# First attention in a fixed order, with row sums from a ones column, and chunks of three tiles, two of them from two batches

## The chip, the cores and the metric

One NeuronCore of one Trainium2 chip. The metric is device time in microseconds (us) of one execution, as the median over runs. TensorE is called PE, VectorE DVE, ScalarE ACT, GpSimd POOL and SyncE, whose queue issues most transfers, SP.

## The reference, cut to what matters

Attention over 4 batches, 8 heads, 768 positions and 64 columns a head, with a window of 128 positions and the first 4 positions as sinks; then a gated MLP without a nonlinearity on the 3072 resulting rows.

```python
scores = scale * np.matmul(q, k.transpose(0, 1, 3, 2))
keep = is_sink | in_window                    # in_window: 0 <= row - col < window
scores = np.where(keep, scores, -1000000000.0)
a = np.exp(scores - np.max(scores, axis=-1, keepdims=True))
a = a / (np.sum(a, axis=-1, keepdims=True) + 1e-09)
attn_out = np.matmul(a, v)                    # (4, 8, 768, 64)
x = attn_out.transpose(0, 2, 1, 3).reshape(B * S, H * D)          # (3072, 512)
return (x @ w_a) * (x @ w_b) @ w_out          # w_a, w_b: (512, 1536), w_out: (1536, 512)
```

The three weights arrive as 64-bit floats.

## The kernel before

The 3072 rows are 24 tiles of 128, six to a batch. The first tile of each batch (t = 0) sees only itself; a later one sees its own block, the block before it and the sinks. The work goes in passes. Ahead of all, `first_tiles` (L405) does the attention of the four first tiles. Then each pass of `moe` (L722) runs the MLP for the rows whose attention is finished, while the attention of the next chunk is fed in between its products, one step of a generator at a time (`between`, L818). `CHUNKS` (L216) lists those chunks as (batch, first tile, tiles); there are eight of 2 or 3 tiles, all of one batch, so there are nine passes: one on the four first tiles and eight on 2 or 3 tiles.

A pass goes over 12 values of j, 128 of the 1536 hidden columns each. For each j, `half` (L730) makes the a and b products, 12 each with as many moving columns as the pass has rows; ACT copies a out of its bank (L755), DVE multiplies it by b (L761), the product is split into a high and a low part (L764, L766), and one j later `project` (L740) adds it to the output banks with three products of 512 columns for each tile (L745). Everything is done in pairs of rounded high and low parts, three products for one, except the attention of the first tiles and of chunk 0 (`parts_exact`, L576), which takes full 32-bit products.

Weights are loaded in the first pass as raw 64-bit words and pass three steps: `weight_bits` (L296: DVE L301 and L303, ACT L302, POOL L305), `weight_high` (ACT L312) and `weight_low` (DVE L317). `weights_to` (L787) calls them one weight behind the other, the second step D1 = 3 weights behind the first and the third D2 = 4 behind it. It is called in `first_tiles` from its seventh `yield` on (nine calls) and three times for each j of the first pass, where at third s it brings the third step to at least s + 3 and goes one weight on at every call.

In `first_tiles`, for each batch: scores of eight heads by products on 64 rows (L417) and a mask product onto each of two banks (L420); the maximum by DVE (L429), the exponentials on ACT with an accumulated row sum (L432), the reciprocal and the scaling of the 512 columns of each half (L438 to L440), transposes (L445) and copies (L446), products with V (L453), and the split into xh and xl (L456, L457). The program's scheduler puts these into an order; instructions under `pin` (`keep_in_program_order`) keep theirs. Eight products on a zero tile (`warm`, L271) stand at the very start.

For a split chunk, `prep_kq` (L351) and `prep_v` (L370) load K, Q and V of a head (K and V for two heads at once) into a ring of six transfer buffers (`io`, L279, NIO = 6), and POOL rounds and subtracts (L343, L346). The weight checks (`check_weight`, L319) load through the same ring, two tiles for each j in which they run, from the third pass on. A buffer is given out again only when its last reader is done, and SP issues in order.

## Time and profile before

| what | us |
|---|---|
| median of 3 runs (823.36 to 824.60) | 824.04 |
| the profiled execution | 823.73 |
| its span, first to last instruction | 821.9 |
| first product of the first MoE pass | 47.87 |
| cut behind the first pass (first split of the next rows, L718) | 174.5 |

The profile of one execution shows each instruction with start and duration. The stages in the rows below are cut at the first MoE product and then at each `split_x` (L718), which starts when the attention of a chunk is finished; the last two projections of a pass still run behind its cut. A matmul's record includes its way through the array, so the records of neighbours overlap; the pace at which they follow each other stands in the chain of waits, which counts every product up to the next one's end.

### The profile page before, as it was taken

The numbers are of one execution on the slowest core, as the hardware profiler recorded it, in microseconds if no ns is written. First come the engines' busy times: TensorE is split into PE (matmuls) and PEld (weight loads), VectorE is DVE, ScalarE is ACT, GpSimd is POOL, SyncE is SP. The second block draws the span as 40 slices with busy tenths as digits, with TensorE's granted clock in tenths as the row PEclk, the third lists the DMA queues.
The fourth block names the chain that finished last, engine by engine and source line by source line (L and its number), as shares of the span: only waits on it lengthen the run. The fifth ranks groups of instructions, "written<-read, shape, count | busy, mean of one in ns | idle before, by whom it ended". The sixth has DMA issues, their size and how long they took to land.

```text
span 821.9 us, 14178 instructions
## 1 busy us (share of the span) xinstructions
PE 789.3 (96%) x4751; PEld 705.0 (86%) x4751; DVE 429.9 (52%) x1365; ACT 476.9 (58%) x1413; POOL 374.8 (46%) x499
## 2 busy tenths in 40 slices
PE   7688999999999999999999999999999999999997
PEld 4466777789889999999999888999998889999996
DVE  4799777426654565335534675355356643442211
ACT  3565666338865777457636886576368755652311
POOL 1244434707762665247363664473646725630110
PEclk7679999999999999999999999999999999999999
DMA  9907510322121332223331443133314211000100
GB/s 337 381 20 280 199 32 4 94 74 66 54 82 39 101 100 91 82 65 116 110 113 52 123 145 96 66 114 115 106 57 137 78 37 54 23 1 1 39 2 29
DMA packets 45662, 76.34 MB, mean 93 GB/s; under 512 B 4688, under 2 KB 25488, under 8 KB 45584
## 3 DMA queue, kind: packets, MB, share of 16 engines
q1 hardware_dynamic: 42384, 69.62, 26.5%
q10 hardware_dynamic: 3168, 5.77, 1.9%
q8 instruction: 38, 0.62, 0.3%
q14 instruction: 40, 0.33, 0.1%
q0 software_dynamic: 32, 0.00, 0.0%
HBM read 69.08 MB, written 6.29 MB: 92 GB/s over the span
## 4 chain that ended last, share of the span: by engine, by line
PE 72%; DVE 11%; ACT 9%; POOL 3%; issue 2%; DMA 2%; SPq 0%; ACTq 0%; POOLq 0%; DVEq 0%
PE b L736 20%; PE o L745 20%; PE a L736 19%; PE t L530 3%; PE s L501 3%; ACT p L508 2%; PE av L545 2%; ACT p L512 2%; DVE pt L534 1%; ACT pt L533 1%; ACT xf L550 1%; DVE xf L551 1%; PE s L417 1%; POOL ks L346 1%; DVE g L761 1%
## 5 line engine op out<-in xcount | busy, mean ns | idle before, releaser
L745 PE MATMUL o<-w_o,gh 128*128 128x512 f32 x576 | 188.2, 407 | 0.0
L736 PE MATMUL b<-xh,w_b 128*128 128x256 f32 (+1 forms) x768 | 186.5, 313 | 0.0
L736 PE MATMUL a<-xh,w_a 128*128 128x256 f32 (+1 forms) x768 | 184.9, 311 | 0.0
L766 POOL TENSOR_TENSOR gl<-g,gh 128x256 fp32r<-128x256 f32 (+1 forms) x80 | 70.2, 878 | 192.6 <-ACT gh L764 188.1
L761 DVE TENSOR_TENSOR g<-b,g 128x256 f32<-128x256 f32 (+2 forms) x108 | 55.4, 513 | 163.0 <-PE b L736 155.4
L736 PEld LDWEIGHTS a<-xh,w_a 128*128 128x128 f32 x768 | 132.3, 188 | 2.3
L736 PEld LDWEIGHTS b<-xh,w_b 128*128 128x128 f32 x768 | 132.3, 188 | 0.0
L736 PE MATMUL b<-xl,w_b 128*128 128x256 f32 (+1 forms) x384 | 118.6, 309 | 0.0
L736 PE MATMUL a<-xl,w_a 128*128 128x256 f32 (+1 forms) x384 | 118.4, 308 | 0.0
L745 PEld LDWEIGHTS o<-w_o,gh 128*128 128x128 f32 x576 | 102.0, 190 | 18.4 <-ACT gh L764 1.1
L745 PE MATMUL o<-w_o,gl 128*128 128x512 f32 x288 | 114.8, 399 | 0.0
L755 ACT COPY g<-a 128x256 f32<-128x256 f32 (+2 forms) x108 | 47.3, 438 | 105.0 <-PE a L736 89.4
L764 ACT CAST gh<-g 128x256 fp32r<-128x256 f32 (+2 forms) x108 | 51.7, 479 | 76.3 <-DVE g L761 74.7
L512 ACT ACTIVATE p<-p,st 128x264 f32<-128x264 f32 x144 | 74.4, 517 | 27.6 <-DVE st L511 27.5
L506 DVE CUSTOM_DVE_ANT_0 p<-s,mg 128x264 f32<-128x264 f32 x120 | 51.3, 427 | 54.0 <-PE s L501 53.4
L534 DVE TENSOR_TENSOR pt<-t,pt 128x256 fp32r<-128x256 f32 x144 | 60.8, 422 | 30.8 <-ACT pt L533 28.8
L508 ACT ACTIVATE p<-p,st 128x264 f32<-128x264 f32 x144 | 74.4, 517 | 3.8 <-DVE st L506 3.6
L736 PEld LDWEIGHTS a<-xl,w_a 128*128 128x128 f32 x384 | 72.3, 188 | 2.2
L736 PEld LDWEIGHTS b<-xl,w_b 128*128 128x128 f32 x384 | 72.3, 188 | 0.0
L346 POOL TENSOR_TENSOR ks<-kr,ks 64x536 fp32r<-64x536 f32 (+1 forms) x56 | 68.0, 1215 | 4.5
L745 PEld LDWEIGHTS o<-w_o,gl 128*128 128x128 f32 x288 | 54.5, 189 | 13.3
L533 ACT CAST pt<-t 128x256 fp32r<-128x256 f32 x144 | 53.4, 371 | 21.3 <-PE t L530 17.1
(153 smaller groups left out, 1424.3 us busy)
## 6 DMA issues: line engine op xcount, KB each, us to landing
raw_a<-in_wa_dram SPq DMA_DIRECT2D x12, 512.0 KB, 7.7
raw_b<-in_wb_dram SPq DMA_DIRECT2D x12, 512.0 KB, 7.8
raw_o<-in_wo_dram SPq DMA_DIRECT2D x12, 512.0 KB, 7.1
qr<-in_qT_dram SPq DMA_DIRECT2D x32, 192.0 KB, 2.8
chk_a<-in_wa_dram SPq DMA_DIRECT2D x24, 256.0 KB, 2.7
chk_b<-in_wb_dram SPq DMA_DIRECT2D x24, 256.0 KB, 2.6
chk_o<-in_wo_dram SPq DMA_DIRECT2D x24, 256.0 KB, 3.0
out_dram<-os ACTq DMA_DIRECT2D x22, 256.0 KB, 2.2
```

Source lines behind the costliest of these rows:

```text
L346: self.nc.gpsimd.tensor_tensor(o, i, high.bitcast(F32), op=ALU.subtract)
L506: nc.vector.tensor_tensor_reduce(out=p[:, :w], in0=ps[:, :w], in1=m, scale=-0.125, scalar=BIG, op0=ALU.add, op1=ALU.min, accum_out=st[:, 0:1])
L508: nc.scalar.activation(p[:, :w], p[:, :w], AF.Exp, bias=st[:, 0:1], scale=-1.0, accum_out=st[:, 1:2])
L512: nc.scalar.mul(p[:, :w], p[:, :w], st[:, 3:4])
L533: nc.scalar.copy(hs, tp[:, :n, :])
L534: nc.vector.tensor_tensor(ls, tp[:, :n, :], hs.bitcast(F32), op=ALU.subtract)
L736: nc.tensor.matmul(ps[:, :n], lhsT=w[:, ksl], rhs=x[:, kk, :n], start=kk == 0 and i == 0, stop=kk == NK - 1 and i == 2)
L745: nc.tensor.matmul(outs[i], lhsT=g[:, sl], rhs=w, start=j == 0 and k == 0, stop=j == NJ - 1 and k == 2)
L755: nc.scalar.copy(g[:, :n], pa[:, :n])
L761: nc.vector.tensor_tensor(g[:, :n], pb[:, :n], g[:, :n], op=ALU.mult)
L764: nc.scalar.copy(gh[:, :n], g[:, :n])
L766: e.tensor_tensor(gl[:, :n], g[:, :n], gh[:, :n].bitcast(F32), op=ALU.subtract)
```

## The change

The attention of the first tiles, `first_tiles`, is written out as one list of calls, and every instruction in it keeps that order. The row sums are no longer accumulated beside the exponentials: V gets two more columns (DA = 66) set to ones, the product is turned (the probabilities are loaded, V moves), its column 64 is the row sum, and the scaling is done on the 64 columns of the result, which then is transposed (`turn`). Twelve products on the zero tile are added (`busy`): two behind the first scores, two ahead of each of two turns, six at the end. K and Q of the next batch are loaded ahead of V of the one before; the ones are set by POOL behind V's transfer. The weights' steps get bounds of their own: in `first_tiles` three first steps, two second and two third; in the passes at third s the first step up to s + 7, the second up to s + 4, at most two at a call, the third up to s + 3. Chunks 1 to 6 have three tiles; the last two take two tiles of one batch and one of another, with K and V in pieces, one sink product for each piece, and eight products of V a head (`PAIR` and `LONE`) where a chunk of one batch has seven (`ROW`). The sink values are loaded at heads 3 and 7 instead of 0 and 4. Small tables share buffers with weights that come late.

The diff, cut to its core:

```diff
-MB = 4
-MK = MB * KB - NS
+MB = 5
+MK = MB * KB - 2 * NS
-CHUNKS = ((0, 1, 2), (0, 3, 3), (1, 1, 3), (1, 4, 2), (2, 1, 3), (2, 4, 2), (3, 1, 3), (3, 4, 2))
+SLOTS = ((0, 4, "BA"), (1, 2, "AB"), (3, 5, "AB"))
+ROW = ((0, 0, 2, 0), (1, 2, 2, 1), (2, 5, 0, 2), (-1, 4, 1, 0))
+PAIR = ((0, 0, 2, 0), (1, 2, 1, 1), (-1, 4, 1, 0))
+LONE = ((0, 5, 0, 2), (-1, 3, 0, 2))
+CHUNKS = (((0, 1, 2),), ((0, 3, 3),), ((1, 1, 3),), ((2, 1, 3),), ((3, 1, 3),),
+          ((1, 4, 2), (2, 4, 1)), ((3, 4, 2), (2, 5, 1)))
+DA = D + 2
...
+    def prep_kq(self, places, h, tag):
+        if h % 2 == 0:
+            self.kr = []
+            for b, t0, n, s0, nb, kw, *_ in places:
+                kr = self.io([P, 4 * KB - NS], F32, f"kr{tag}_{h}_{b}")
+                self.nc.sync.dma_start(kr[:, :kw], self.kT[b, h // 2, :, s0 * KB:s0 * KB + kw])
+                self.kr.append(kr)
...
+        for b in range(B + 1):
...
+            if b:
+                nc.sync.dma_start(self.vs0[b - 1], self.v0[b - 1])
+                nc.gpsimd.memset(self.vs0[b - 1][:, :, D:], 1.0)
...
+        def busy(bank, n):
+            for _ in range(n):
+                pin(T.matmul(bank, lhsT=self.z[:, :P], rhs=self.z[:, :bank.free_size()], start=True, stop=True,
+                             skip_group_check=True))
...
+        def exps(b, e):
             for pr in range(NP):
-                A.activation(p[:, pr, :], s[:, pr, :], AF.Exp, bias=st[:, 1, pr:pr + 1], scale=0.125,
-                             accum_out=st[:, 2, pr:pr + 1])
+                pin(A.activation(ps[b][:, e, pr, :], banks[b][e][:, pr, :], AF.Exp,
+                                 bias=sts[b][:, 1, e, pr:pr + 1], scale=0.125))
...
         def av(b):
+            avs[b] = [tile(("av", "o2")[e], [P, NP, DA], f"av0_{b}_{e}") for e in range(2)]
+            for e in range(2):
+                for pr in range(NP):
+                    pin(T.matmul(avs[b][e][:, pr, :], lhsT=pts[b][:, e, pr, :], rhs=self.vs0[b][:, 2 * pr + e, :],
+                                 start=True, stop=True))
+
+        def scale(b):
+            st = sts[b]
+            for e in range(2):
+                pin(V.tensor_scalar(st[:, 2, e], avs[b][e][:, :, D], 1e-9, None, op0=ALU.add))
+            pin(V.reciprocal(st[:, 3], st[:, 2]))
+            for e in range(2):
+                pin(V.tensor_tensor(xs[b][:, :, e, :], avs[b][e][:, :, :D],
+                                    st[:, 3, e].unsqueeze(2).to_broadcast([P, NP, D]), op=ALU.mult))
+
+        def turn(b, n):
+            xts[b] = tile(("t", "s", "o0", "s")[b], [P, NP, P], f"xt0_{b}")
+            busy(xts[b].rearrange("p a b -> p (a b)"), n)
             for pr in range(NP):
+                pin(T.transpose(xts[b][:, pr, :], xs[b][:, pr].rearrange("p a b -> p (a b)"), self.ident))
...
+        scores(0)
+        busy(tile("t", [P, DM], "busy0"), 2)
+        mask(0)
+        top(0, 0)
+        top(0, 1)
+        scores(1)
+        mask(1)
+        exps(0, 0)
...
+        av(3)
+        scale(3)
+        turn(2, 2)
+        split(2)
+        between(2)
+        turn(3, 2)
+        busy(tile("t", [P, DM], "busy1"), 6)
+        split(3)
+        between(3)
...
+        def beside(k):
+            if k == 0:
+                weights(load=3, bits=1)
+            elif k == 1:
+                weights(load=9, bits=2, high=1)
+                next(gen)
+            elif k == 2:
+                weights(load=9, bits=2, high=2, low=1)
+            elif k == 3:
+                weights(load=9, bits=3, high=2, low=2)
...
             def ahead(s):
                 j = s // 3
-                weights_to(max(s + AHEAD, done[0] + 1 - D2), LOADS)
+                weights(load=s + LOADS + AHEAD, bits=min(s + AHEAD + D2, done["bits"] + 2),
+                        high=min(s + AHEAD + 1, done["high"] + 2), low=s + AHEAD)
```

## Rows read from the trace of the kernel before

**Rows 1.** The page: busy time, share of the span and instructions of each engine (part 1), and the clock that PE was granted in 40 equal slices, in tenths (part 2).

```profile
PE 789.3 (96%) x4751; PEld 705.0 (86%) x4751; DVE 429.9 (52%) x1365; ACT 476.9 (58%) x1413; POOL 374.8 (46%) x499
...
PEclk7679999999999999999999999999999999999999
```

**Rows 2.** The chain of waits, pieces in order of time: start in us, length in us, engine, tile, line and count. The first is of the pass on four tiles, the next two of a pass on three, the last two of the pass on two.

```profile
101.02 2.79 PE o L745 x12
...
340.27 2.08 PE a L736 x12
...
344.44 4.19 PE o L745 x18
...
765.59 1.41 PE a L736 x12
...
779.79 1.40 PE o L745 x6
```

**Rows 3.** Busy time of each engine in each stage, in us, with the count of instructions, the granted clock, the busy share of the transfer engines and GB/s. The first is the first attention, the next two the first MoE pass; 174.5 and 597.5 start passes on two tiles beside attention of three, 251.1 one on three beside three.

```profile
0.00:47.87 47.87, 33.34 (x176) 22.92 (x176) 30.65 (x76) 24.76 (x88) 10.54 (x17) 0.69 0.83 311
47.87:80.00 32.13, 29.30 (x113) 22.37 (x113) 31.14 (x53) 17.64 (x37) 15.54 (x13) 0.87 0.45 160
80.00:174.50 94.50, 93.25 (x438) 72.69 (x437) 60.58 (x135) 52.55 (x117) 39.65 (x40) 1.00 0.27 86
174.50:251.10 76.60, 74.40 (x535) 68.62 (x534) 43.25 (x160) 52.82 (x164) 46.24 (x62) 1.00 0.22 68
251.10:344.50 93.40, 93.17 (x551) 87.16 (x551) 49.13 (x176) 60.71 (x187) 47.16 (x62) 1.00 0.29 89
...
597.50:673.80 76.30, 73.48 (x528) 67.14 (x527) 44.19 (x177) 53.51 (x171) 44.52 (x62) 1.00 0.27 82
```

**Rows 4.** The timeline, instructions in order of time: start in us, length in us, engine, line, operation, result and sources, shape and count, and in brackets the idle time before it and what ended it.

```profile
4.81 1.20 PE L417 MATMUL s<-kq 64*128 64x128 f32 x16
...
5.99 0.35 DVE L265 SCALAR_TENSOR_TENSOR m<-col,nw_val,mg 128x128 bf16<-128x128 f32 x1
...
6.97 0.23 DVE L269 TENSOR_SCALAR mg<-rel,nw_val 128x8 f32<-128x8 f32 x1
...
10.46 1.65 PE L420 MATMUL s<-m,identb 128*128 128x512 bf16 x4
...
23.98 1.97 PE L453 MATMUL av<-pt,v 128*64 128x128 f32 x14
...
25.88 1.97 PE L445 MATMUL t<-ident,p 128*128 128x128 f32 x8
...
30.01 1.09 PE L453 MATMUL av<-pt,v 128*64 128x128 f32 x14
...
41.07 1.29 POOL L305 TENSOR_TENSOR wf_b<-wf_b,raw_b 128x512 int32<-128x512 int32 x1 [3.58 <-ACT raw_b L302]
...
44.72 0.69 DVE L303 SCALAR_TENSOR_TENSOR wf_o<-raw_o,wf_o 128x512 int32<-128x512 int32 x1
...
48.56 0.42 DVE L301 TENSOR_SCALAR wf_b<-raw_b 128x512 int32<-128x512 int32 x1
...
50.94 1.52 POOL L305 TENSOR_TENSOR wf_b<-wf_b,raw_b 128x512 int32<-128x512 int32 x1 [0.78 <-ACT w_a L312]
...
51.24 1.52 DVE L301 TENSOR_SCALAR wf_o<-raw_o 128x512 int32<-128x512 int32 x1
...
816.02 0.39 PE L745 MATMUL o<-w_o,gl 128*128 128x512 f32 x1
```

**Rows 5.** Groups of instructions by line and shape, here POOL's subtraction of K for a chunk of three tiles and one of two: count, busy us, mean ns of one, idle us before them.

```profile
L346 POOL TENSOR_TENSOR ks<-kr,ks 64x536 fp32r<-64x536 f32 x32 | 42.9, 1342 | 2.6
...
L346 POOL TENSOR_TENSOR ks<-kr,ks 64x400 fp32r<-64x400 f32 x24 | 25.1, 1046 | 1.9
```

**Rows 6.** The chain of waits at the start.

```profile
2.23 6.17 DMA kq<-in_kq_dram
...
8.45 2.08 PE s L417 x16
...
11.11 1.29 DVE st L429 x2
...
12.57 1.29 ACT p L432 x7
```

**Rows 7.** Groups by line and shape in the first attention, 0 to 47.87 us: count, busy us, mean ns of one, idle us before them.

```profile
L432 ACT ACTIVATION_READ_ACCUMULATOR p<-s,st 128x1 f32 x32 | 7.3, 227 | 0.0
...
L440 DVE TENSOR_TENSOR p<-p,st 128x512 f32<-128x512 f32 x8 | 6.4, 799 | 0.1
...
L429 DVE TENSOR_REDUCE st<-s 128x4 f32<-128x512 f32 x8 | 5.4, 686 | 5.3 <-PE s L420 5.3
...
L438 DVE TENSOR_SCALAR st<-st 128x4 f32<-128x4 f32 x8 | 1.2, 159 | 2.7 <-ACT p L432 2.7
```

**Rows 8.** Busy time of each engine in stretches of 4 us, with the granted clock (1.00 is 2.4 GHz, 0.50 is 1.2).

```profile
16.00:20.00 4.00, 4.00 (x16) 2.68 (x15) 3.09 (x10) 2.62 (x16) 0.00 (x0) 0.50 1.03 410
...
24.00:28.00 4.00, 4.00 (x24) 3.34 (x24) 2.44 (x6) 2.17 (x10) 0.00 (x0) 0.50 1.02 408
```

**Rows 9.** What SP's queue waited for in the pass from 251.1 to 344.5 us (us in total, times, longest), and then the transfers by line: KB each and median us from issue to landing.

```profile
SPq L333 <- POOL ql L346: 34.5, 6, 18.4
...
kr<-in_kT_dram SPq DMA_DIRECT2D x16, 268.0 KB, 2.7
```

More of the change, by code (lines that the diff above doesn't have):

```diff
@@ L33 @@
 NIO = 6
-STEP0 = 7
 AHEAD, LOADS = 3, 9
-D1, D2 = 3, 4
+D2 = 4
 WARM = 8
@@ L392, in first_inputs @@
[L392 to L394 removed]
+        self.kqs = [self.wp.tile([P, NP, 2, P], F32, tag=HOMES[b], name=f"kq{b}") for b in range(B)]
+        self.vs0 = [self.wp.tile([P, H, DA], F32, tag=HOMES[B + b], name=f"v0_{b}") for b in range(B)]
+        for b in range(B + 1):
             if b == 0:
@@ L459, in first_tiles @@
[L459 to L475 removed]
+            pin(A.copy(xh[:, :, cols], xts[b]))
@@ new lines, in split @@
+            pin(V.tensor_tensor(xl[:, :, cols], xts[b], xh[:, :, cols].bitcast(F32), op=ALU.subtract))
+        scores(0)
[6 more added lines that the diff above has]
+        exps(0, 0)
+        top(1, 0)
+        exps(0, 1)
+        transposes(0, 0)
+        top(1, 1)
+        exps(1, 0)
+        transposes(0, 1)
+        exps(1, 1)
+        scores(2)
+        mask(2)
+        top(2, 0)
+        top(2, 1)
@@ new lines, in first_tiles @@
+        av(0)
+        scale(0)
+        transposes(1, 0)
+        exps(2, 0)
+        between(0)
+        transposes(1, 1)
+        scores(3)
+        mask(3)
+        exps(2, 1)
+        top(3, 0)
+        top(3, 1)
+        turn(0, 0)
+        split(0)
+        av(1)
+        exps(3, 0)
+        scale(1)
+        transposes(2, 0)
+        transposes(2, 1)
+        exps(3, 1)
+        av(2)
+        turn(1, 0)
+        between(1)
+        scale(2)
+        transposes(3, 0)
+        transposes(3, 1)
@@ new lines, in first_tiles, with attention @@
+        split(1)
+        av(3)
[7 more added lines that the diff above has]
+        between(3)
+    def attention(self, segs, xf, exact=False):
+        tiles = [t0 + i for _, t0, n in segs for i in range(n)]
+        nt = len(tiles)
+        late = [i for i, t in enumerate(tiles) if t >= 2]
+        parts = self.parts_exact(*segs[0], xf) if exact else self.parts_split(segs, tiles, late, xf)
@@ L840, in run @@
                     pass
-                rows = [nb * S + (nt0 + i) * P for i in range(nnt)]
-                xs = self.split_x(nxf, nnt, f"{rows[0]}")
+                rows = nrows
+                xs = self.split_x(nxf, len(rows), f"{rows[0]}")
         return val, self.ok
```

262 lines of the change are left out of this document (119 added, 143 removed).

## The prediction

> **What bounds the kernel now.** I read the page first: TensorE (PE) is busy for 96% of the span and its granted clock is below full only in the first three of the 40 slices [rows 1]. A busy PE is not a PE at its pace, because records overlap, so the next view is the chain of waits, which gives the pace: a half of twelve products takes 1.41 us on two tiles and 2.08 us on three, the projection of one j takes 1.40 us and 4.19 / 2 = 2.10 us, and 2.79 us on the first four tiles [rows 2]. One j of the MoE alone is therefore 2 x 1.41 + 1.40 = 4.22 us on two tiles (12 j: 50.7) and 2 x 2.08 + 2.10 = 6.26 us on three (75.1): 25.4 us a tile against 25.0. The width of a chunk hardly matters to the products themselves.
>
> The table of stages [rows 3] then shows three regimes. To 47.87 us the first attention runs, and no MoE product. From 47.87 to 174.5 the first MoE pass splits the weights beside it; up to 80 us VectorE (DVE) is busy 31.14 of 32.13 us, so the weights set the time there, and behind 80 us PE does (93.25 of 94.50). From 174.5 to the last product at 816.4 [rows 4] PE sets it. That last stretch is 641.9 us: four passes on two tiles (202.8), four on three (300.4), the two last projections of the first pass, which end behind the cut (2 x 2.79 = 5.6), and so 133.1 us of attention and waits. By pass, with the projections that each cut moves: three tiles of attention beside two MoE tiles cost 76.6 - 50.7 - 5.6 + 2.8 = 23.1 us, and in the pass from 597.5 76.3 - 50.7 - 4.2 + 2.8 = 24.2; three beside three cost 93.4 - 75.1 - 2.8 + 4.2 = 19.7; the last pass has none [rows 2, 3]. The same attention costs 4 us more where the MoE beside it is short.
>
> **Merging the chunks.** Eight chunks (2, 3, 3, 2, 3, 2, 3, 2) become seven (2, 3, 3, 3, 3, 3, 3). MoE: 50.7 + 6 x 75.1 = 501.3 instead of 503.2. Attention: 23.1 for the first (unchanged), 3 x 19.7 for the three of one batch, and two mixed ones. A mixed chunk has eight products of V a head instead of seven and doubled sink products; one product more is half as wide, an estimate of 0.6 us a chunk from the pace above. Its preparation on GpSimd (POOL) is dearer: K comes in two pieces, 400 and 264 columns instead of 536. By [rows 5] the subtraction falls from 1342 to 1046 ns for 136 columns less, so 264 cost some 750; with the rounding, V's two pieces and Q as now I estimate 6.0 us a head instead of 4.7. In the pass of three beside three POOL is busy 47.16 of 93.4 us (0.50), in that of three beside two 44.52 of 76.3 (0.58) [rows 3]; 8 x 1.3 us more make 57.6 of 93.4 (0.62). So a mixed chunk stands nearer to the short passes, which wait 4 us. Its wait is bounded by 0 and 4.5 us; I take 2, between, since no chunk of two batches is in the trace. Attention after: 23.1 + 59.1 + 2 x 22.3 = 126.8 instead of 133.1. With 501.3 - 503.2 the sum is **-8.2 us**, bounds -12.2 and -3.2. The last pass has three tiles to store instead of two; the third copy is ScalarE's (ACT), whose first is done by then: nothing, at most one more copy.
>
> **The first attention.** Now the first product on loaded data is followed by the second batch's scores, which wait for a transfer that lands at 8.40; the mask products of batch 0 stand behind them and the first maximum starts at 11.11, the first exponential at 12.57 [rows 6]. The mask itself is ready at 5.99 + 0.35 = 6.34, and the scores at 6.0 [rows 4]. In the fixed order the mask follows its own scores, so the exponentials begin near 8.1: 4.4 us earlier. Row sums by the ones column take the accumulator reads away (32, 227 ns each, though part of each lies under the next instruction: seven records take 1.29 us, so an exponential goes every 0.34) and the scaling of 512 columns before the transposes (8 x 0.80) [rows 6, 7]. In their place stand two reads of PSUM and two half-wide multiplications a batch, four transposes, and 12 products on zeros.
>
> Each engine's sum, all pinned in order: DVE, from 7.2 when the masks are done, has 8 maxima with their step (0.69 + 0.16), 4 scalings (two small steps, a reciprocal, two of some 0.42: 1.35), 4 copies and 4 subtractions over as many columns, three weights' first step (0.42 + 0.69) and two last ones (0.69) [rows 4, 7]: 6.8 + 5.4 + 5.5 + 3.3 + 1.4 = 22.4, so 29.6 at the earliest. ACT has less. PE depends on its clock. At full clock a batch is 1.20 of scores, 0.43 of masks (four took 1.65 at half clock), half of 1.97 for eight transposes (those were at half clock), 1.09 x 16 / 14 = 1.25 of V, 0.5 to turn: 4.4, four of them and the zeros (12 at 0.21) 20. At half clock it is 2.08, 0.83, 1.97, 2.25, 1.0: 8.1, with the zeros (0.41 each) 37.4 [rows 4]; from 4.8 that ends at 42.2, with a few waits 44. So the first MoE product moves from 47.9 to between 30 and 44. In the trace the clock was half between 16 and 28 although PE was busy without a gap [rows 8]: scores on 64 rows did not lift it. The new order has the full-array transposes and V products denser, and zeros only at both ends. I take full to 12, half to 25, full again: half of those 13 us is lost, less what DVE hides, 5.5 on 30: **35.5, -12.4 us** (bounds -17.9 and -3.9).
>
> A page speaks against the turned V product. The Trainium skill (TensorE: Matmul & The Clock Gate, LDWEIGHTS) says that a weight load takes its columns over 1.2 GHz, 107 ns for 128; V now moves 66 columns on 128 loaded ones, so by an estimate from it 16 passes take 1.7 us where I have 1.25. That would make PE 1.8 us longer in all, and the time 808.2 if none of it were hidden; the trace has 12 products with 12 such loads in 1.41 us, 118 ns apart, and cannot tell the two. The sum above does without it.
>
> **The first pass and its weights.** Before, nine weights had their first step, six the second and five the third when the pass began; after, 3, 2 and 2. That moves six first steps and three last ones into the pass: 6 x 1.11 + 3 x 0.69 = 8.7 us of DVE, and 6 x 1.29 of POOL [rows 4]. Against it the lead asked for shrinks by three weights at every third of a j (three times DVE's 1.80 and POOL's 1.29: 9.3), and the half clock that the pass now begins in may be gone. From 80 us on DVE has room (60.58 of 94.5 busy) [rows 3]; what is exposed is the burst at the start, where the second pair of halves needs weight 3, behind five first steps. DVE's pinned steps stand ahead of the multiplication that frees PE's bank. I take **+3 us**, bounds -2 and +14.
>
> The upper bound comes from the port. A first step lasts 0.42 us at 48.56 but 1.52 at 51.24, where POOL's addition had begun at 50.94 [rows 4]: it ends when POOL's does. If every weight is that serial (0.42 + 0.69 + 0.69 + 1.29 = 3.1 us), the five that stand before the first multiplication need 15.5 us where PE's two halves need 5.5, and the two asked for at the next third, in which the first j has no projection, some 4 us more than the attention there hides: 14. The Trainium skill (GPSIMD Engine Reference, Specifications) says that GpSimd shares its SBUF interfaces with VectorE and contends with instructions of two SBUF inputs. By that rule the last two steps would be held as well; the trace has the rule for the first step, and the time by it is the second rival's.
>
> **Sum.** 821.9 - 8.2 - 12.4 + 3.0 = 804.3 of span; the profiled execution took 823.73, 1.8 more than its span: 806.1; the median of the runs, 824.04, is 0.3 above it: **806.4 us**.
>
> **Rivals.** (1) All goes together: the clock holds (-17.9), the first pass loses nothing, mixed chunks do not wait (-12.2): 821.9 - 30.1 + 2.1 = 793.9. For it: DVE's sum ends at 29.6. Against: PE at half clock in [rows 8]. (2) The port holds the weights: +14 instead of +3 gives 817.4. For it: DVE full to 80 us. Against: the shorter lead. (3) The zeros do not do what they are for: the clock is half throughout, 44 instead of 35.5, 814.9. For it, again [rows 8]; against it, the full-array work. (4) Slower than before: the ring of six transfer buffers. In a mixed chunk an even head takes five of them (two K, Q, two V), and the weight checks two for each j. SP issues in order; already a check's load waited for POOL's release 34.5 us in sum in the pass from 251.1, 18.4 at once, with the next head's loads behind it on that queue [rows 9]. If the K and V loads of a pair are issued only as POOL frees them, their time, 2.7 us each to land [rows 9], comes bare on PE, whose scores stand in order ahead of MoE products: two such trips are 5.4 us, over 2 x 4 pairs 43 in place of the 4 that I count: 845. From 2.7 us a pair on (21.6 / 8) the change is a loss. Against it: the scores need a head's K only some 8.6 us after its preparation may start (93.4 / 36 thirds x 3.3). (5) Nothing: gains and losses cancel, 824.
>
> **Chances.** Forecast (798 to 812) 0.40; (1) 0.22; (2) 0.12; (3) 0.14; (4) 0.07; (5) 0.05. Faster by over 0.2%, about what a measurement of this kernel tells from no change, is the first four: 0.88; within it 0.05; slower 0.07. The range runs from 790, below (1), to 819, above (2) and (3): it leaves (4), (5) and some of the edges out.
>
> **What would show it.** The first MoE product near 35, with the half clock between 12 and 25; the first exponential near 8; a first pass of some 130 us whose early multiplications wait behind weight steps on DVE; passes of three beside three of 93 us, mixed ones of 95 to 96, the last of 75 and the tail. A first product behind 42, a first pass over 137, or mixed passes over 98 would each show the step wrong that I named.

## The result and the profile after

The changed kernel takes **800.14 us** (median; 799.74 to 805.68) against 823.7 for the kernel before: ratio 0.9728, 95% interval 0.9691 to 0.9766, so 2.3 to 3.1% faster. 806.4 had been forecast. The profiled execution is the slowest of the runs, 805.68 us with a span of 803.8, 18.1 less than before; its mean granted clock is 0.987, where the other runs show 0.996 to 0.997.

The page's busy line and its row of the granted clock, to be read beside [rows 1]:

```profile
PE 784.0 (98%) x4503; PEld 703.9 (88%) x4503; DVE 427.5 (53%) x1321; ACT 467.2 (58%) x1341; POOL 383.3 (48%) x513
...
PEclk9699999999999999999999999999999999999999
```

Of the first three slices, all clearly below full clock before, only the second still is.

Busy time by stage, the columns of [rows 3]: the first attention, the first MoE pass in two parts, the pass on two tiles, three passes of three beside three, two mixed passes (from 522.8), the last pass with the tail.

```profile
0.00:36.43 36.43, 33.31 (x204) 24.83 (x205) 22.45 (x62) 17.39 (x47) 5.17 (x17) 0.81 0.90 339
36.43:70.00 33.57, 27.87 (x113) 20.34 (x111) 32.47 (x54) 19.32 (x40) 17.93 (x13) 0.95 0.52 182
70.00:164.10 94.10, 93.59 (x438) 73.01 (x439) 70.35 (x144) 55.67 (x124) 44.32 (x41) 1.00 0.30 96
164.10:240.30 76.20, 74.29 (x535) 68.51 (x534) 43.17 (x160) 52.73 (x165) 46.29 (x62) 1.00 0.25 75
240.30:333.60 93.30, 93.07 (x551) 87.13 (x550) 49.08 (x176) 60.49 (x186) 48.93 (x62) 1.00 0.31 94
333.60:428.20 94.60, 94.37 (x558) 88.47 (x557) 49.27 (x176) 61.22 (x188) 48.94 (x62) 1.00 0.32 96
428.20:522.80 94.60, 94.37 (x558) 88.43 (x557) 49.68 (x176) 61.36 (x188) 51.73 (x70) 1.00 0.31 93
522.80:620.60 97.80, 96.94 (x571) 89.89 (x570) 50.54 (x176) 62.80 (x196) 60.61 (x98) 1.00 0.33 102
620.60:718.70 98.10, 96.81 (x571) 89.94 (x570) 48.77 (x177) 59.30 (x179) 49.19 (x78) 1.00 0.19 57
718.70:803.80 85.10, 79.42 (x415) 73.31 (x414) 11.69 (x22) 16.92 (x34) 10.17 (x10) 0.98 0.05 20
```

From the timeline, the last product:

```profile
797.73 0.39 PE L830 MATMUL o<-w_o,gl 128*128 128x512 f32 x1
```

So the last product ends at 798.1 (816.4 before [rows 4]), and the 18.1 us of span divide into four pieces. The first MoE product moved from 47.87 to 36.43: -11.4. The first pass went from 126.6 to 127.7: +1.0. From its end to the last product it was 641.9 us and is 634.0: -7.9. The tail is 0.2 longer. Forecast were -12.4, +3.0, -8.2 and nothing.

The first attention in the timeline (idle time and what ended it in brackets), four instructions of it:

```profile
7.23 0.59 PE L451 MATMUL s<-flat 128*128 128x512 bf16 x2 [0.45 <-DVE flat L267]
...
7.95 0.68 DVE L455 TENSOR_REDUCE st<-s 128x4 f32<-128x512 f32 x1
...
8.94 3.20 ACT L460 ACTIVATE p<-s,st 128x128 f32<-128x128 f32 x12 [5.77 <-PE s L442]
...
12.96 1.90 PE L473 MATMUL av<-v,pt 128*128 128x66 f32 x16
```

The mask products no longer stand behind the second batch's scores: the first maximum starts at 7.95 instead of 11.11, the first exponential at 8.94 instead of 12.57 [rows 6]. Twelve exponentials come in a row, with no accumulator reads between them. Then the clock, in stretches of 4 us with the columns of [rows 8]:

```profile
16.00:20.00 4.00, 3.53 (x38) 3.08 (x34) 3.90 (x9) 2.76 (x10) 1.28 (x1) 1.00 1.03 409
20.00:24.00 4.00, 3.08 (x20) 2.88 (x20) 3.55 (x10) 3.04 (x9) 0.00 (x0) 0.81 1.04 395
24.00:28.00 4.00, 4.00 (x20) 3.76 (x19) 1.29 (x5) 1.05 (x3) 1.28 (x1) 0.50 1.03 398
28.00:32.00 4.00, 4.00 (x19) 3.53 (x19) 1.86 (x6) 0.05 (x1) 0.00 (x0) 0.50 0.91 350
32.00:36.00 4.00, 4.00 (x15) 2.54 (x14) 2.45 (x6) 2.26 (x4) 0.00 (x0) 0.50 0.58 198
```

The clock is full to 22.5 us while PE waits a little (3.53 and 3.08 of 4 us busy in the first two stretches), falls there, and stays at 1.2 GHz for 13.7 us (22.5 to 36.1) although PE is busy without a gap from 24 on: the same sight as in [rows 8], later. The busy share is itself higher at half clock, because the same products take longer: sixteen of V 3.65 us at 27.66, where they take 1.90 at 12.96.

### The profile page after: what moved, and what is told of

It reads as the page before. It is cut to its first block, busy times and chain, and to the rows that moved or that the text cites. A ratio compares the mean times of both kernels' runs of the same rounds, so it can differ in the third digit from the quotient of the medians.

```text
span 803.8 us, 13543 instructions
## 1 busy us (share of the span) xinstructions
PE 784.0 (98%) x4503; PEld 703.9 (88%) x4503; DVE 427.5 (53%) x1321; ACT 467.2 (58%) x1341; POOL 383.3 (48%) x513
## 4 chain that ended last, share of the span: by engine, by line
PE 81%; DVE 7%; ACT 5%; POOL 3%; DMA 2%; issue 1%; SPq 0%; POOLq 0%; ACTq 0%; DVEq 0%
PE o L830 22%; PE a L821 22%; PE b L821 21%; PE t L612 4%; PE s L584 4%; PE av L627 3%; ACT p L591 1%; PE av L473 1%; PE t L743 1%; DMA kr<-in_kT_dram 1%; POOL ks L343 1%; ACT xf L632 1%; PE sk L654 1%; PE s L705 1%; DMA qr<-in_qT_dram 1%
## 5 line engine op out<-in xcount | busy, mean ns | idle before, releaser
L821 PE MATMUL a<-xh,w_a 128*128 128x384 f32 (+1 forms) x672 | 183.0, 335 | 0.0
L821 PE MATMUL b<-xh,w_b 128*128 128x384 f32 (+1 forms) x672 | 181.7, 334 | 0.0
L851 POOL TENSOR_TENSOR gl<-g,gh 128x384 fp32r<-128x384 f32 (+1 forms) x70 | 68.2, 974 | 170.8 <-ACT gh L849 169.7
L846 DVE TENSOR_TENSOR g<-b,g 128x384 f32<-128x384 f32 (+2 forms) x96 | 53.4, 556 | 171.8 <-PE b L821 140.2
L821 PEld LDWEIGHTS a<-xh,w_a 128*128 128x128 f32 x672 | 120.8, 188 | 1.2
L821 PEld LDWEIGHTS b<-xh,w_b 128*128 128x128 f32 x672 | 120.4, 188 | 0.0
L821 PE MATMUL b<-xl,w_b 128*128 128x384 f32 (+1 forms) x336 | 110.2, 328 | 0.0
L821 PE MATMUL a<-xl,w_a 128*128 128x384 f32 (+1 forms) x336 | 110.1, 328 | 0.0
L849 ACT CAST gh<-g 128x384 fp32r<-128x384 f32 (+2 forms) x96 | 49.3, 514 | 73.6 <-DVE g L846 71.8
L840 ACT COPY g<-a 128x384 f32<-128x384 f32 (+2 forms) x96 | 45.1, 469 | 77.6 <-PE a L821 66.7
```

Of the source, the lines that this page charges most:

```text
L821: nc.tensor.matmul(ps[:, :n], lhsT=w[:, ksl], rhs=x[:, kk, :n], start=kk == 0 and i == 0, stop=kk == NK - 1 and i == 2)
L840: nc.scalar.copy(g[:, :n], pa[:, :n])
L846: nc.vector.tensor_tensor(g[:, :n], pb[:, :n], g[:, :n], op=ALU.mult)
L849: nc.scalar.copy(gh[:, :n], g[:, :n])
L851: e.tensor_tensor(gl[:, :n], g[:, :n], gh[:, :n].bitcast(F32), op=ALU.subtract)
```

## The experiments

Theory: the gain has two parts that do not depend on each other, a first attention that ends some 12 us earlier because of its order and its shorter chains, and passes that all run at the pace of three beside three; the clock of the start sets how much of the first part arrives. Rivals: the zeros do it or do nothing; the accumulators do it; mixed passes lose on the ring of transfer buffers; VectorE's weights, held by GpSimd, take the gain back in the first pass.

The first is the changed kernel again, the other eleven are edits of it. The kernel before was measured again beside them: median 823.22 beside e1 to e4, 824.56 beside e5 to e8, 822.8 beside e9 to e12. One table for all: median of the runs with its ratio to before and the interval; then, of the profiled execution alone, the start X of the first MoE product, the length of the first pass, and the half clock ahead of X, in us.

| kernel | median | ratio (95%) | X | first pass | half clock |
|---|---|---|---|---|---|
| before | 823.7 | 1 | 47.9 | 126.6 | 29 |
| changed | 800.14 | 0.9728 (0.9691-0.9766) | 36.4 | 127.7 | 13.7 |
| e1_again | 801.21 | 0.9724 (0.9694-0.9753) | 33.2 | 128.5 | 6.8 |
| e2_no_zeros | 799.93 | 0.9711 (0.9682-0.9741) | 30.5 | 127.8 | 0 |
| e3_first_only | 808.18 | 0.9823 (0.9793-0.9854) | 29.7 | 128.5 | 0 |
| e4_chunks_only | 813.07 | 0.9875 (0.985-0.99) | 45.8 | 126.2 | 24 |
| e5_accumulate | 803.86 | 0.9762 (0.9736-0.9787) | 34.0 | 128.5 | 6.8 |
| e6_alike | 796.65 | 0.9665 (0.963-0.9701) | 33.2 | 128.5 | 6.8 |
| e7_long_lead | 807.93 | 0.979 (0.9762-0.9817) | 33.6 | 134.0 | 6.8 |
| e8_late_steps | 806.97 | 0.9792 (0.9763-0.9821) | 33.2 | 131.3 | 6.8 |
| e9_add_on_dve | 796.29 | 0.9687 (0.9669-0.9705) | 33.3 | 120.2 | 6.8 |
| e10_one_step | 828.08 | 1.0053 (1.0035-1.0071) | 33.1 | 143.6 | 6.8 |
| e11_one_no_zeros | 824.61 | 1.0031 (1.0013-1.0049) | 30.3 | 143.5 | 0 |
| e12_unpinned | 806.6 | 0.9787 (0.9754-0.9821) | 38.2 | 127.8 | 10.2 |

**The changed kernel again.** No edit.

> The changed kernel as it is, a second time. Its profiled execution took 805.7 us and had PE at half clock from 22.5 to 36.1 us; its other runs took 799.7 to 800.5 with a higher mean clock. Theory: the 6 us between them are the clock of the first attention, which falls in some executions and not in others. An execution near 800 then shows full clock up to the first MoE product, and that product at 30 to 31 us instead of 36.4; the passes behind it are as long as in the first profile (127.7, 76.2, 93.4, 94.6, 94.6, 97.8, 98.2, 79.4 within 1). Rival: the first attention is as long in every execution and the 6 us lie in the first pass, where the weights wait for transfers: then the first product stays near 36 and the first pass shrinks to 122.

Measured: 801.21. Its profiled execution had the half clock for 6.8 us ahead of X, half as long as the first profile, and X came 3.2 us earlier. X is thus no fixed number of this kernel, and what follows compares profiles that had the same half clock, or says what they had.

**Without the zeros.**

```diff
-            for _ in range(n):
+            for _ in range(0):
```

> The 12 products on zeros are left out; nothing else. Theory: they hold the clock, and without them PE is at half clock for most of the first attention in every execution: the first MoE product at 38 to 44 us, the time 807 to 813. Rival: the full-array products of the new order hold the clock alone and the zeros only cost their own 2.5 us: the first product at 28 to 31, the time 798 to 801. Between: they matter at the end alone, where the six last ones raise the clock for the first MoE products: 802 to 805.

Measured: 799.93, 0.13% from e1 by the ratios and inside its interval; the theory fell, and the numbers are the first rival's. The profile has no half clock at all ahead of X, and X is 30.5. Busy time of e2 in three stretches of 4 us:

```profile
20.00:24.00 4.00, 2.77 (x23) 2.57 (x24) 3.73 (x12) 3.04 (x10) 0.00 (x0) 1.00 1.04 397
24.00:28.00 4.00, 3.71 (x34) 3.50 (x34) 2.74 (x8) 1.43 (x3) 1.29 (x1) 1.00 1.04 403
28.00:32.00 4.00, 2.39 (x12) 1.42 (x11) 3.70 (x9) 2.26 (x4) 0.00 (x0) 1.00 1.03 397
```

PE is less busy here than in the changed kernel from 24 to 32, and yet granted the full clock throughout; 34 products run from 24 to 28 where the changed kernel had 20. This execution also shows what the first attention costs when the clock is full. Pieces of its chain of waits from 4 to 32 us (start, length, engine, result, line, count):

```profile
11.80 1.09 PE s L442 x16
12.89 0.54 PE s L451 x2
13.43 1.75 PE av L473 x16
...
18.68 0.82 DVE st L456
...
22.32 1.97 PE av L473 x16
...
25.89 1.98 PE av L473 x16
...
28.33 0.76 DVE x L482 x2
```

Three of the four groups of V products are on the chain, 5.7 us, 20.4% of these 28 us. Sixteen products start 108 to 113 ns apart at full clock; a group takes 1.75 us where other products follow, and up to 1.98 where its result is waited for, which includes the last one's way through the array. Counted were 1.25.

**Each part alone.** The old eight chunks with the new first attention, and the new chunks with the old first attention. Of the first:

```diff
+TWO = ((0, 0, 2, 0), (1, 2, 0, 1), (-1, 4, 1, 0))
...
-CHUNKS = (((0, 1, 2),), ((0, 3, 3),), ((1, 1, 3),), ((2, 1, 3),), ((3, 1, 3),),
-          ((1, 4, 2), (2, 4, 1)), ((3, 4, 2), (2, 5, 1)))
+CHUNKS = (((0, 1, 2),), ((0, 3, 3),), ((1, 1, 3),), ((1, 4, 2),), ((2, 1, 3),), ((2, 4, 2),),
+          ((3, 1, 3),), ((3, 4, 2),))
...
-            groups = [(k + 1, *rest) for k, *rest in ROW]
+            groups = [(k + 1, *rest) for k, *rest in (ROW if nt == 3 else TWO)]
```

> The new first attention and the new bounds of the weights, but the eight old chunks. Theory (two independent parts): the chunks are worth 8 us and the rest 15.5, so 808 where the clock holds, 814 where it falls; the passes behind the first as in the kernel before (76.6, 93.4, 89.3, 76.0, 87.7, 76.3, 87.6, 55.0). Rival: the parts overlap (the earlier start moves transfers or weights onto the passes behind): 803 or below.

Measured: 808.18, 15.0 below before. Passes two to nine take what they took before (end of the first pass to the last product 642.1 us, 641.9 before), so all of it is the start: X 29.7, the first pass 128.5.

Of the second the edit is long: the inputs, first tiles and lead of weights of the kernel before, in the new chunk list.

> The new chunks, but the first attention, its loads and the bounds of the weights as before. Theory: -8 us, 815.7, with the first MoE product near 47.9 and a first pass near 126.6 as before, mixed passes near 98. Rival (the chunks give more beside the old first part, or the new place of small tables and the later load of the sinks change it): below 812 or above 820.

Measured: 813.07, 10.2 below. From the end of the first pass to the last product 633.2 us: 8.7 less than before, in e1 8.8. The two parts make 25.2 us together where the whole makes 22.0. In per cent that is 3.0 against 2.8, inside e1's interval (2.5 to 3.1), so the sum is not told from the whole. In the profiles the difference stands at X and goes with the clock: e3's had no half clock ahead of it, e1's had 6.8 us; and e4's X of 45.8 is 2.1 below before, with 24 us of half clock instead of 29.

**Row sums by the accumulator again**, with the ones column left in use (the extra result is read by nobody):

```diff
-                                 bias=sts[b][:, 1, e, pr:pr + 1], scale=0.125))
+                                 bias=sts[b][:, 1, e, pr:pr + 1], scale=0.125,
+                                 accum_out=sts[b][:, 3, e, pr:pr + 1]))
```

> The changed kernel, but each exponential also accumulates its row sum into a spare column, as before; the sum is not used. It gives back the 32 accumulator reads alone. Theory: ScalarE is not what ends the first attention (its busy time there is 16.9 of 30.5 us in the run without zeros), so the first MoE product stays within 1 us of the 30 that it has at full clock (up to 36 where the clock falls), and the time at 800 to 801.5. Rival: the reads stand on the chain from scores to transposes, 4 batches x 8 reads x 0.09 us and more: the first product 3 us later, 803 to 804.

Measured: 803.86. At the same half clock X is 34.0 instead of 33.2, and the profiled executions, both at a mean clock of 0.993, differ by 1.5 us (803.86 and 802.32); the medians differ by 2.7. The 32 reads add 8.3 us of busy time to ACT, and 0.8 of it shows at X: ACT does not set the end of this stage. X is thus the theory's; the time is nearer the rival's, with an interval that overlaps e1's, and the other 0.8 us of the profiles lie behind the first pass, where the edit does nothing.

**Tiles of one batch in the last two chunks.** It leaves out tiles 4 and 5 of batch 1 and computes tile 3 of batches 2 and 3 twice, so that two passes of three beside three stand where the mixed ones stood (the expectation also names tile 4 of batch 3 as left out; it is computed):

```diff
-          ((1, 4, 2), (2, 4, 1)), ((3, 4, 2), (2, 5, 1)))
+          ((2, 3, 3),), ((3, 3, 3),))
```

> The two chunks of two batches are replaced by two of one batch (tiles 3 to 5 of batches 2 and 3), so tiles 4 and 5 of batch 1 and tile 4 of batch 3 are not computed and others twice; as many tiles, sinks and passes. What is left of a difference is the price of mixing. Theory: 3.2 us a pass, 1.3 of it the eighth product and the second sink products, the rest waits on POOL's longer preparation: the two passes fall from 97.7 to 94.5, the time by 6.4 to 794. Rival: the wait is on the ring of transfer buffers, which the weight checks share; then the first of the two passes, with checks in eight of its j, gains more than the second, with four: by over 1 us.

Measured: 796.65. The two passes take 95.2 and 95.0 where e1 has 97.7 and 97.3: a mixed chunk costs 2.4 us, 4.8 for both (2.6 each were forecast, 2 of them waiting). The first pass, which has more of the weight checks beside it, gains 2.5 and the second 2.3, not over 1 us apart as the rival of the ring had it. If the ring of six buffers were what costs, waits of PE on K and Q would also have to be there. What SP's queue waited for in the first mixed pass of the changed kernel (us in sum, times, longest), as in [rows 9], and then the only line in which PE's queue waited for K there:

```profile
SPq L335 <- POOL ql L343: 19.0, 2, 17.3
SPq L366 <- POOL ks L343: 12.3, 4, 6.2
```

```profile
PEld s L584 <- POOL ks L343: 0.4, 1, 0.4
```

SP waits for POOL for long, as it did before, and 0.4 us of it reaches PE. PE's own idle time in that pass is 0.86 us (96.94 busy of 97.80), POOL is busy 60.61 of 97.80 (0.62, as forecast). So most of the 2.4 us is no wait on the ring. Busy time of PE and of its weight loads on V's products alone (L627) in the first of the two passes, in e1 and then in e6:

```profile
520.40:618.10 97.70, 8.87 (x64) 8.09 (x64) 1.00 0.33 101
```

```profile
520.50:615.70 95.20, 7.43 (x56) 7.30 (x56) 1.00 0.30 95
```

Counted in the traces from each product's start to the next one's, V's products take 8.1 and 7.8 us in the two passes of e1 and 6.3 in those of e6, and the scores 6.7 and 6.8 instead of 6.3 and 6.2. At the pace of e6 (0.113 us) the eight more products are 0.9 us; what is left of these differences, some 1.2 us, is time spent between products.

**The lead of the weights, longer and shorter.** First a lead like that of the kernel before:

```diff
-                weights(load=s + LOADS + AHEAD, bits=min(s + AHEAD + D2, done["bits"] + 2),
-                        high=min(s + AHEAD + 1, done["high"] + 2), low=s + AHEAD)
+                high = min(s + AHEAD + 4, done["high"] + 2)
+                weights(load=s + LOADS + AHEAD, bits=min(s + AHEAD + D2 + 3, done["bits"] + 2),
+                        high=high, low=min(s + AHEAD + 3, high))
```

> The lead of the weights' steps in the first pass as long as before (first step up to 10 weights on, second 7, third 6, at most two first and second steps at a call), all else as in the changed kernel. Theory: what the pass loses by beginning with three weights instead of nine it gets back by asking for less; with the long lead three more weights (1.80 us of VectorE and 1.29 of GpSimd each) stand ahead of the first multiplications, and the first pass takes 5 to 9 us more than 128: 806 to 810. Rival: the lead is not what the first j wait for, and the pass stays within 1.5 us of 128.

Measured: 807.93, the first pass 134.0, 5.5 more than e1's; its profile has one stretch of half clock (3.4 us) more in that pass, which can account for at most 1.7 of it. PE's waits from X to the end of the pass, first of e7 and then of e1 (us in sum, times, longest):

```profile
PE s L705 <- DVE st L709: 5.0, 3, 2.2
```

```profile
PE s L705 <- DVE st L709: 1.1, 2, 1.0
```

In sum, PE's waits for weights fall from 4.2 us to 0.9 and those for the attention's steps rise from 2.5 to 9.3: the weights' steps that come earlier stand ahead of the attention's on VectorE, and PE waits for those. Then, one first step a call instead of two:

```diff
-                weights(load=s + LOADS + AHEAD, bits=min(s + AHEAD + D2, done["bits"] + 2),
+                weights(load=s + LOADS + AHEAD, bits=min(s + AHEAD + D2, done["bits"] + 1),
```

> At most one weight has its first step at a call, instead of two, so the lead of 7 is never reached and stays at 4. Theory (the long lead cost 5.5 us because steps stand ahead of VectorE's multiplication): three first steps fewer ahead of the first multiplications, the first pass 2 to 4 us shorter than 128.3, the time 797 to 799. Rival: the first j wait for the weights themselves, whose chain runs over VectorE, GpSimd, ScalarE and VectorE again; a shorter lead then makes each weight late and the pass 1 to 5 us longer.

Measured: 828.08, 0.35 to 0.71% slower than the kernel before. The first pass is 143.6 and the pass after it 86.3 instead of 76.3. Busy time of e10 at the start of the first pass, and in the pass after it:

```profile
33.10:70.00 36.90, 32.48 (x134) 23.98 (x133) 24.91 (x58) 21.48 (x48) 12.69 (x11) 0.95 0.71 250
176.70:262.90 86.20, 76.67 (x528) 69.31 (x527) 46.44 (x161) 52.74 (x165) 56.12 (x73) 0.96 0.24 73
```

and what PE waited for longest in both passes together:

```profile
PE a L821 <- ACT w_a L314: 9.3, 9, 2.0
```

VectorE is busy only 24.91 of 36.90 us: the burst is gone, but at one step for each third of a j a weight's chain ends only when PE wants it, PE waits for it again and again, and weights are still split in the next pass. My theory, that the burst at the start costs PE and spreading it gains, fell with this run: the lead must be built up early, and two steps a call do that.

**No zeros on top of that**, as a second pair on what they do:

```diff
-            for _ in range(n):
+            for _ in range(0):
```

> The same with the 12 products on zeros left out. Theory: the zeros do nothing for the clock nor for the time, so this is e10 within 1.5 us, with the clock falling in some executions and not in others, as with them. Rival: without zeros the clock falls more often (half clock over 6 us in the profile, 2 us more than e10).

Measured: 824.61 against 828.08, ratios 1.0031 and 1.0053 with intervals that overlap, so no difference is told, though the medians are 3.5 us apart where 1.5 was expected. Again no half clock ahead of X (30.3), but 3.4 us of it just behind.

**Attention's steps eight thirds later in the first pass**, so that VectorE starts it with weights alone:

```diff
-                want = min(steps, -(-steps * (s + 1) // (3 * NJ - 3)))
+                late = 0 if c else 8
+                want = min(steps, -(-steps * max(s + 1 - late, 0) // (3 * NJ - 3 - late)))
```

> In the first pass the steps of the attention beside it begin at the ninth third of a j instead of the first and then go faster; the same work in all. Theory: up to 70 us VectorE sets the time (38.4 of 39.5 us busy between 30.5 and 70 in the run without zeros), and each step of that attention takes some 0.8 us of it; with seven steps moved behind that stretch the first pass shrinks by 3 to 5 us, the time to 796 to 798. Rival: the stretch is bound by the weights' own chain over three engines, the steps fill gaps of VectorE, and moving them makes the later part longer: the pass stays at 128 or grows.

Measured: 806.97, the first pass 131.3, 2.8 more. VectorE is busy 35.42 of the first 36.80 us, against 35.66 in e1, but does 44 instructions instead of 61: the attention's 20 small ones (4.0 us in e1) are gone and only three weight steps more are done. The others got longer (the first step of b's weights, L303, 975 ns instead of 415), so no time was gained, and the work put off is missing later. That the steps had filled gaps, as the rival says, does not show in VectorE's busy time; why the others got longer was not tried.

**The addition on VectorE.** The last whole-number addition of each weight moves from GpSimd to VectorE, so that VectorE has more to do and no addition of GpSimd's runs beside it:

```diff
-        nc.gpsimd.tensor_tensor(f, f, lo, op=ALU.add)
+        nc.vector.tensor_tensor(f, f, lo, op=ALU.add)
```

> The weights' addition (L307) is done by VectorE instead of GpSimd (there it may round the 32-bit integers); nothing else. It tests the second rival: whether the first j of the first pass wait because VectorE is held while GpSimd adds. In the run without zeros, 30.5 to 70 us, the group means say that VectorE's weight steps and splits last some 12 us longer than at their shortest (0.42 and 0.69), and 13 additions run on GpSimd. Theory (held): 13 additions of 0.69 are 9 us more for VectorE, 12 less are held: the first pass shrinks from 128 by 2 to 5 us, time 796 to 799. Rival (VectorE is simply full, and a held instruction would have waited anyway): the pass grows by 3 to 8 us, time 804 to 809.

Measured: **796.29**, the fastest of the kernels that compute the whole reference, and faster than both kernels of this case. The first pass is 120.2 us, 8.3 less than e1's and 7.6 less than e2's; e1 has a stretch of half clock there (3.4 us), e2 and e9 have none. The start of the first pass in e1, and then in e9:

```profile
33.20:70.00 36.80, 30.02 (x123) 21.80 (x122) 35.66 (x61) 21.08 (x46) 19.19 (x14) 0.95 0.65 233
```

```profile
33.30:70.00 36.70, 35.56 (x159) 27.51 (x158) 35.47 (x85) 26.91 (x59) 4.11 (x3) 1.00 0.80 286
```

VectorE is busy as long as before, but does 85 instructions instead of 61 in that time; PE is busy 35.56 instead of 30.02. Groups by line and shape from 33 to 120 us (count, busy us, mean ns of one, idle time before), the same lines of e1 and then of e9:

```profile
L319 DVE TENSOR_TENSOR w_a<-wf_a,w_a 128x512 fp32r<-128x512 f32 x9 | 9.0, 1000 | 0.1
...
L851 DVE TENSOR_TENSOR gl<-g,gh 128x512 fp32r<-128x512 f32 x7 | 7.5, 1066 | 3.2 <-ACT gh L849 3.2
...
L303 DVE TENSOR_SCALAR wf_a<-raw_a 128x512 int32<-128x512 int32 x9 | 7.1, 784 | 0.0
...
L846 DVE TENSOR_TENSOR g<-b,g 128x512 f32<-128x512 f32 x7 | 4.8, 684 | 0.5 <-PE b L821 0.5
```

```profile
L307 DVE CUSTOM_DVE_ANT_0 wf_a<-raw_a,wf_a 128x1024 uint16<-128x1024 uint16 x9 | 6.2, 687 | 1.0 <-ACT raw_a L304 0.7
...
L319 DVE TENSOR_TENSOR w_a<-wf_a,w_a 128x512 fp32r<-128x512 f32 x9 | 6.1, 678 | 0.0
L851 DVE TENSOR_TENSOR gl<-g,gh 128x512 fp32r<-128x512 f32 x8 | 5.5, 688 | 0.8 <-ACT gh L849 0.8
L846 DVE TENSOR_TENSOR g<-b,g 128x512 f32<-128x512 f32 x8 | 5.5, 684 | 0.4 <-PE b L821 0.4
...
L303 DVE TENSOR_SCALAR wf_a<-raw_a 128x512 int32<-128x512 int32 x9 | 3.8, 418 | 0.0
```

Without GpSimd's additions the same instructions take 678, 688 and 418 ns instead of 1000, 1066 and 784. Three kinds of them were held, not the first step alone; the multiplication L846, which reads one of its two inputs from PSUM, takes 684 ns in both. The addition itself is 687 ns on VectorE, where it had been some 1440 on GpSimd, so each weight's chain over the engines is some 0.75 us shorter as well; how much of the gain is that was not tried by itself. At the median the gain is smaller than in the profiles: 0.37% by the ratios, some 3 us, with intervals that overlap a little (0.9705 and 0.9694), and 4.9 by the two medians. Behind the first pass 1.5 us of the 8.3 are lost again (634.6 us to the last product against 633.1); why was not tried.

**The new arithmetic without the fixed order.** The products, reads and small steps of the first tiles are left for the scheduler to place:

```diff
-        nc, pin = self.nc, self.tc.keep_in_program_order
+        nc, pin = self.nc, lambda x: x
```

> The new first attention with its new operations, but its instructions are not pinned: the program's scheduler orders them again. It tells the order from the arithmetic. Theory: the gain of the first attention is the order (the mask behind its own scores, the first exponential 3.6 us earlier, three batches in flight); without it the first MoE product comes at 40 us or later and the time is 806 or more. Rival: the gain is the arithmetic (scaling 256 columns instead of 1024, no accumulator reads) and the few weights: the first product stays at 30 to 36 us, the time at 799 to 803.

Measured: 806.6, 5.4 above e1, X 38.2. The first exponential in its timeline:

```profile
10.63 3.21 ACT L460 ACTIVATE p<-s,st 128x128 f32<-128x128 f32 x12 [7.46 <-DVE st L456]
```

It starts at 10.63: 1.7 later than with the order fixed, 1.9 earlier than before. Of the 14.7 us between before's X and e1's, 5.0 go with the order; the other 9.7 are there without it (new arithmetic, order of loads, fewer weights ahead, and less half clock). X came between what the theory and the rival expected, the time is the theory's. The half clock ahead of X is 10.2 us in this profile, 6.8 in e1's and 29 before, so some of the 5.0, and much of the 9.7, is clock.

## Why the prediction was right

**What bounds.** Behind the first pass PE set the time, as read from [rows 2, 3]: the passes keep their lengths where their content is the same (76.2 and 93.3 after, 76.6 and 93.4 before; e3's old chunks give 642.1 in all against 641.9, one pass 1.2 longer with 3.4 us of half clock in it and one 0.7 shorter).

**Merging: -8.2 forecast, -7.9 in the first profile, -8.8 and -8.7 in e1 and e4.** The step that carried it, that attention costs 19.7 us beside three MoE tiles and 23 to 24 beside two, is right: the passes of 94.6 less the MoE's 75.1 leave 19.5. A mixed pass was given 22.3 and takes 97.8 - 75.1 = 22.7 and 23.0 (e1: 22.6 and 22.2). The half width of one product was estimated at 0.6 and the wait at 2 us; the count of e6 says that the split between the two was off: 0.9 for the eight more products, some 1.2 us between products, and 0.3 not assigned. The 0.4 to 0.6 by which e6's passes are longer than 94.6 has nothing to do with mixing: in tiles 3 to 5 three tiles have products with the sinks, in tiles 1 to 3 two, and those products and their transposes (L654, L641) take 1.5 us instead of 1.0 in the traces. One sign did not follow from the prediction's own sum, mixed passes of 95 to 96: 75.1 and 22.3 make 97.4. In the first profile the second of them, 98.1, is just past the 98 that was to show the step wrong; the first (97.8) and e1's (97.7, 97.3) are not.

**The first attention: X at 35.5 forecast, 36.4 in the first profile, 33.1 to 34.0 in most, 29.7 to 30.5 at full clock (e2, e3, e11).** The bounds were 30 and 44, and the lower one is a measured case now. The chain of starts came as forecast but for 0.8 us (first exponential 8.9 for 8.1; the small transfer that the mask waits for had landed at 4.7 us before and lands at 5.6). The step that took X from 30 to 35.5 assumed 13 us of half clock between 12 and 25 and gave 5.5 us for it. The price is about right: 13.7 us cost 36.4 - 30.5 = 5.9, and 6.8 us cost 33.2 - 30.5 = 2.7 (0.8 more each against e3's 29.7). The stretch was mis-sized: it starts at 21 to 23 and is mostly 6.8 us long, not 13. That is the mis-sized term, and with it goes that the profiled execution (805.68) lies by the forecast and the median 6.3 us under it. The mean clock says so for the runs without a trace: a clock of 0.987 over 803.8 us is 2 x 0.013 x 803.8 = 20.9 us of half clock, one of 0.9965 over 798 us is 5.6, what falls at the very end of the span included (some 1 to 3.4 us in the traces). That the first profile's span came within 0.5 us of the forecast 804.3 is thus in part luck: its half clock happened to last 13.7 us. Nor was the reason given for the old half clock, scores on 64 rows, shown: the stretch from 24 to 28 in [rows 8] holds transposes on 128 rows too [rows 4], and the new order stays at half clock through its V products and transposes on 128 rows.

How much of the move of X is clock and how much the new order and arithmetic is not separated by any run. Before, 29 us ahead of X were at half clock (a granted clock of 0.69 over 47.87 us, [rows 3]). On the old first attention 5.6 us less of it went with 2.1 us less of X (e4), on the new one 6.8 and 13.7 us cost 2.7 and 5.9. By an estimate from these (0.37 to 0.43 us for each) the old 29 us cost 11 to 13 of the 17.4 us between 47.9 and 30.5, and 5 to 7 would be left at an equal clock. Why the new first attention has less half clock was not tried either; with the order left to the scheduler e12 has 10.2 us, with the old first attention e4 has 24.

**The turned V product** was mis-sized the other way: 1.25 us counted, 1.75 to 1.98 measured on the chain, and three of four such groups lie on the chain in e2. About 2 us of the first attention were thus counted too low. The Trainium skill (TensorE: Matmul & The Clock Gate, LDWEIGHTS) has a load of 128 columns at 107 ns, by an estimate from it 1.7 us for sixteen; the trace agrees, with 108 to 113 ns from one product to the next at full clock. VectorE's sum came out: of the 22.4 us forecast from 7.2 on, 19.9 lie ahead of X in e2, and the last subtraction, one first and one last step of the weights, 2.5 us, behind it, and the first MoE product did not wait for them.

**The first pass: +3 forecast, +1.0 to +1.9 measured** (127.7 to 128.5 against 126.6). The old pass had 8.2 us of half clock in it, e2's none and the others' 3.4, so at an equal clock the moved steps cost somewhat more than that. That the shorter lead would pay for the steps moved into the pass is borne out: a longer one costs 5.5 more (e7). That it could be spread out further fell (e10: +15, and +10 in the next pass).

**The rivals.** (1), 793.9, had the full clock and X near 30, which exist (e2), but also a first pass and mixed chunks without loss, which do not. (2), the port: its mechanism is borne out and its price, +14, was wrong. With GpSimd's additions gone VectorE's last steps are shorter as well as its first (e9: 678 instead of 1000 ns, 418 instead of 784). The Trainium skill (GPSIMD Engine Reference, Specifications) says that VectorE's instructions contend with GpSimd when they have two SBUF inputs or run in a 2-port mode; the trace agrees for the two-input ones, and L846 with one input in PSUM is not slowed. But the additions run beside VectorE in the kernel before too [rows 4], so the hold is no cost of the change. It was not tried there what taking them away brings. (The held first step of [rows 4] ends at 52.76, 0.3 us behind GpSimd's addition and not with it.) (3): its premise is half borne out. Without the zeros no difference in time is told (e2 and e1, e11 and e10, intervals overlapping both times, the kernel without them lower in both). What it concluded, half clock throughout and 814.9, is wrong: the two profiles without zeros had none ahead of X. Whether the zeros even bring the half clock on is open: of nine profiles with zeros and the fixed order, eight have it from 21.2 to 22.7 on and one (e3) has none, the two without have none; but the mean clocks of the timed runs are alike, 0.992 to 0.997 for e1 and 0.991 to 0.999 for e2. (4), the ring: SP does wait, 0.4 us reach PE, and e6 gains as much in the pass with few weight checks as in the one with many. (5) is out.

## What to carry to other kernels

Read the price of a stage by the pass and by what stands beside it, not by the tile: the same attention cost 4 us less beside longer MoE work, and that sum held within 0.6 us. Where VectorE is full, look for a GpSimd instruction that runs beside it before counting its instructions: moving work onto the full engine made the first pass 8 us shorter here (VectorE did 85 instructions in the time of 61). Where the clock changes from one execution to the next, count the half clock of both kernels before a shorter stage is put down to its order. A start that runs at either clock needs its sum at both, and more than one profiled execution, since one of them may be the slowest of the runs.

## What the runs showed that was not expected

The same kernel had 6.8 or 13.7 us of half clock ahead of its first MoE product, and the clock stayed at 1.2 GHz through stretches in which PE was busy 4.00 of 4 us (24 to 36, at the longer products of half clock), while an execution with PE busy 2.39 to 3.71 of 4 us kept 2.4 GHz (20 to 32 in e2). Products on zeros moved the time by nothing that two pairs of kernels could tell.

VectorE's 128x512 steps with two inputs in SBUF took 0.78 to 1.07 us in the mean of a group and those with one 0.54 to 0.78 while GpSimd added, 0.68 to 0.69 and 0.42 without it, and the addition of whole numbers on VectorE appeared in the trace as an operation on 128x1024 values of 16 bits, in 0.687 us.
